# A quarter of a weight matrix decoded earlier, and lasting staging rooms, in a fused attention and two-MoE kernel

## The chip, the cores and the metric

One core of a Trainium2 chip runs the whole program. Engines are called as in the profile: PE (TensorE), DVE (VectorE), ACT (ScalarE), POOL (GpSimd), SP (SyncE, whose queue here issues all the large transfers). The metric is device time in microseconds (us) of one execution; lower is better.

## The reference

Three blocks follow each other; shapes are batch 4, 8 heads, S = 576, 2304 tokens of width 512.

```python
scores = q @ k.T / 8 + bias(pos)              # bias: small MLP of log distances, per head
x = softmax(scores) @ v                       # -> 2304 x 512
g = x @ w_gate; y = (silu(g) * (x @ w_val)) @ w_out       # MoE 1, 512 -> 1536 -> 512
h = relu(y @ w_in); out = (h * h) @ w_out2                # MoE 2, 512 -> 2048 -> 512
```

All tensors come as float64 in DRAM; the kernel sees the weights as pairs of 32-bit words.

## The kernel before, in words

**Stages.** Attention walks query tiles t = 0, 1, 2, 3 of 128 rows each and then a merged tile "m", made of the last 64 rows of two batches at a time. MoE 1 runs in nine units of 256 tokens, moe1(0) to moe1(8), mostly beside attention: per unit 12 steps f of 24 matmuls 128x128 by 128x256 (L460, gate and value), after each f a tanh on ACT (L468), two products on DVE (L469, L471) and, one step later, a cast on ACT (L445) and its remainder on POOL (L220); then 72 matmuls with the output weights (L483, "z times o"). MoE 2 follows for chunks of two units: hidden() is 192 matmuls (L1381) with elementwise work on ACT, POOL and DVE, outputs() is a scheme of 7 products (L1413) on combined weight blocks.

**Weights.** A weight block is 128 rows by 512 columns, 512 KB in DRAM. SP loads it raw into a staging room (`Source.load`, L283), DVE turns the word pairs into float32 with three instructions (`decode`, L262, L265, L267), ACT or POOL squares it and PE sums the squares for a norm (`first`, L328), and then `split` makes two float16 parts of it (L191 on DVE, L201, L205, L209 on ACT, L197 on POOL). w_in of MoE 2 has four column quarters of four blocks each, w_out2 has sixteen blocks (`second`, L361 for the squares). Quarters 0 and 1 of w_in are decoded in attention's merged tile, through rooms in `scrap`, into `room0` (w2a). When attention is over its pool is given back (`a_stack.close()` in `weights2`); a new pool holds `w2r` (25 blocks), `w2s` (three raw rooms) and `w2c`. Quarters 2 and 3 and then w_out2 pass through the three rooms. With all norms known, `combine(f)`, eight times, scales two blocks of w_out2 (L1212 on POOL, L1214 on ACT), takes differences (L1193) and casts (L1198 DVE, L1200 ACT) into C7. The hidden values of a chunk go to HS, MoE 1's outputs come back transposed as `yt` (`yt_load`, L1231), which in program order waits until gate and value of unit 8 are through, `("gv", 8)`.

**Tiles.** `room1` holds the score biases of an attention tile and `scrap` small tables and raw rooms; both belong to attention's pool before. In the merged tile only the first 4 S columns of `room1` hold biases, which the last softmax step (L823) of the tile reads.

**Order.** Generators for attention, weights and MoE 1 hand out costs at each `yield`; a merge with a table LEAD decides whose turn is next, and a scheduler then orders the instructions of each engine. Each engine runs its own queue in order. PSUM banks of MoE 1's steps: two buffers `mm`, and from the point where `w2r` exists every third step takes the single buffer `ma`.

## Time and profile before

| what | us |
|---|---|
| median of 3 runs | 1247.36 |
| lowest, highest | 1241.97, 1256.09 |
| profiled execution, its own time | 1245.34 |
| span of its trace | 1241.8 |
| PE busy | 1094.9 (88%) |
| DVE busy | 784.5 (63%) |
| ACT busy | 679.2 (55%) |
| POOL busy | 655.5 (53%) |
| mean granted TensorE clock | 0.954 |

The span runs from the first to the last instruction; the time has 3.5 us around it. PE is busiest over the whole, but a share of the whole mixes stages, so the rows below go stage by stage. Times in rows are us from the span's start. The merged tile runs from about 655 to 760, unit 7 from 751 to 806, unit 8 from 806 to 875, the first chunk of MoE 2 to 963.

### The profile page before, as it was taken

Reading aid. Unit: us, or ns where it says so; the run is one execution under the profiler, and the core shown is the slowest. Engines: PE = TensorE matmul, PEld = TensorE weight load, DVE = VectorE, ACT = ScalarE, POOL = GpSimd, SP = SyncE. Lnnn points to the kernel's source line nnn. Section 1 sums busy time; section 2 is a strip of 40 time slices with the busy share of each in tenths; the row PEclk is TensorE's granted clock in tenths of the full one; section 3 lists DMA queues with packets and bytes.
Section 4 is the critical chain, followed back from the end, with each engine's and each line's share of the span. In section 5 each row is a group of like instructions: output and inputs, shape, how many; then the busy total and the mean of one; then the engine's idle time right before and its main releaser. Section 6 shows DMA issues by size and latency. Waiting matters only on the chain.

```text
span 1241.8 us, 27334 instructions
## 1 busy us (share of the span) xinstructions
PE 1094.9 (88%) x10550; PEld 816.1 (66%) x10550; DVE 784.5 (63%) x1864; ACT 679.2 (55%) x1370; POOL 655.5 (53%) x835
## 2 busy tenths in 40 slices
PE   2587799998778889999997999979969999999998
PEld 2566688686467568686774767556438476584787
DVE  5989857887677667666665745885772442624423
ACT  3567767557566566566663543367551643616433
POOL 2433213279768587778794452227890542705423
PEclk9779899999879999999999999989979999999999
DMA  9957543219999998997989995660010010010100
GB/s 226 258 135 206 178 132 87 50 57 200 218 211 202 225 214 171 222 195 156 196 172 245 241 225 134 213 188 1 17 34 18 18 43 26 18 35 17 27 27 17
DMA packets 278078, 163.20 MB, mean 131 GB/s; under 512 B 233276, under 2 KB 246588, under 8 KB 277948
## 3 DMA queue, kind: packets, MB, share of 16 engines
q1 hardware_dynamic: 277948, 161.46, 55.4%
q8 instruction: 82, 1.34, 0.5%
q14 instruction: 48, 0.39, 0.1%
HBM read 92.13 MB, written 19.48 MB: 90 GB/s over the span
## 4 chain that ended last, share of the span: by engine, by line
PE 46%; DMA 15%; DVE 10%; POOL 8%; ACT 5%; issue 3%; SPq 1%; POOLq 0%; ACTq 0%; DVEq 0%
PE mm L1381 12%; PE mm L460 12%; PE mm L1413 11%; DMA pT<-pt 3%; PE mm L483 3%; POOL pt L220 2%; PE av L876 2%; PE ma L1413 2%; DMA qT<-qs 2%; PE qk L814 2%; DMA w2s<-in_moe_w_out_dram 2%; DMA scrap<-in_moe_w_in_dram 1%; POOL zx L1193 1%; DMA wr<-in_v_dram 1%; DMA w2s<-in_moe_w_in_dram 1%
## 5 line engine op out<-in xcount | busy, mean ns | idle before, releaser
L460 PEld LDWEIGHTS <-wr 128*128 128x128 f16 x2592 | 252.6, 100 | 52.8 <-issue 16.5
L1193 POOL TENSOR_TENSOR zx<-zx 128x256 f32<-128x256 f32 (+1 forms) x160 | 141.6, 895 | 181.6 <-ACT zx L1390 176.1
L460 PE MATMUL mm<-xT,wr 128*128 128x256 f16 x1536 | 184.1, 275 | 10.8 <-DVE th L471 5.2
L220 POOL TENSOR_TENSOR pt<-s,pt 128x512 f16<-128x512 f32 x224 | 173.6, 798 | 32.0 <-ACT pt L838 27.9
L220 POOL TENSOR_TENSOR zx<-th,zx 128x256 f16<-128x256 f32 x108 | 81.2, 754 | 129.9 <-ACT zx L445 126.0
L483 PE MATMUL mm<-wr,zx 128*128 128x512 f16 x612 | 142.3, 379 | 1.3 <-DVE th L471 1.3
L823 DVE CUSTOM_DVE_ANT_0 s<-qk,room 128x576 f32<-128x576 f32 x144 | 107.6, 748 | 40.2 <-PE qk L814 20.2
L1413 PEld LDWEIGHTS <-wr 128*128 128x128 f16 x1134 | 112.3, 99 | 27.0 <-DVE wr L1193 4.9
L1193 DVE TENSOR_TENSOR wr<-zx,wr 128x768 f16<-128x768 f32 (+3 forms) x60 | 78.3, 1312 | 61.9 <-ACT wr L1200 60.8
L831 ACT ACTIVATE s<-s,sc 128x576 f32<-128x576 f32 x112 | 85.5, 771 | 55.3 <-DVE sc L830 44.3
L460 PE MATMUL mm<-zx,wr 128*128 128x256 f16 x864 | 104.7, 278 | 2.4 <-DVE th L471 2.4
L606 DVE TENSOR_TENSOR scrap<-scrap,room 128x1024 f16<-128x1024 f16 (+1 forms) x108 | 87.8, 826 | 25.5 <-PE ma L645 21.3
L483 PEld LDWEIGHTS <-zx 128*128 128x128 f16 x648 | 60.1, 98 | 66.0 <-issue 2.4
L1381 PE MATMUL mm<-wr,room 128*128 128x512 f16 (+1 forms) x480 | 100.0, 358 | 0.0
L1381 PE MATMUL mm<-wr,w2r 128*128 128x512 f16 (+1 forms) x480 | 99.9, 358 | 0.0
L622 POOL TENSOR_TENSOR scrap<-scrap 128x256 f32<-128x256 f32 (+1 forms) x90 | 64.1, 713 | 65.9 <-ACT scrap L621 62.4
L876 PE MATMUL av<-vp,pT 128*128 128x65 f16 (+3 forms) x1792 | 70.5, 196 | 28.4 <-DMA pT<-pt 25.0
L876 PEld LDWEIGHTS <-pT 128*128 128x128 f16 (+1 forms) x1792 | 61.8, 102 | 43.5 <-DMA pT<-pt 33.2
L1432 ACT ACTIVATE ob<-ob,fac 128x256 f32<-128x256 f32 x36 | 17.8, 506 | 109.3 <-DVE ob L1431 109.3
L645 PEld LDWEIGHTS <-scrap 128*128 128x128 f16 x1440 | 60.3, 105 | 26.3 <-issue 11.9
L1381 PEld LDWEIGHTS <-w2r 128*128 128x128 f16 x480 | 47.0, 98 | 46.4
L1381 PEld LDWEIGHTS <-room 128*128 128x128 f16 x480 | 47.0, 98 | 45.5
(290 smaller groups left out, 2213.8 us busy)
## 6 DMA issues: line engine op xcount, KB each, us to landing
kp<-kT_d SPq DMA_DIRECT2D x64, 288.0 KB, 3.5
vp<-v_d SPq DMA_DIRECT2D x48, 325.0 KB, 3.5
w2s<-in_moe_w_out_dram SPq DMA_DIRECT2D x16, 512.0 KB, 3.9
wr<-in_moe_w_gate_dram SPq DMA_DIRECT2D x24, 256.0 KB, 5.0
wst<-in_moe_w_out_dram SPq DMA_DIRECT2D x12, 512.0 KB, 3.7
wr<-in_moe_w_val_dram SPq DMA_DIRECT2D x24, 256.0 KB, 4.2
...
```

The lines of the kernel that those rows point to most:

```text
L220: nc.gpsimd.tensor_tensor(out=out_, in0=x, in1=hi, op=ALU.subtract)
L460: nc.tensor.matmul(pg[:, 256 * gi:256 * gi + 256], wr.parts(key, f // 4, cc, wl, P * (f % 4), P), mov(xl, cc), start=k == 0, stop=k == 11)
L483: nc.tensor.matmul(po, zall[:, f, zl, P * t:P * t + P], wr.parts("o", 0, f, wl), start=k == 0, stop=k == 3 * NF1 - 1)
L606: nc.vector.tensor_tensor(out=m[:, :, ni * e:ni * e + ni], in0=block(kb, i0, ni), in1=th, op=ALU.is_gt)
L622: nc.gpsimd.tensor_tensor(out=tmp[r], in0=tmp[r], in1=xb, op=ALU.mult)
L645: nc.tensor.matmul(pv[:, :, :, c:c + 4], m[:, a, :], bd[:, l], start=l == 0, stop=l == 1)
L823: nc.vector.tensor_tensor_reduce(out=s.rearrange("p (a j) -> p a j", a=2), in0=pq[:, :, 0:288], in1=bias[:, n].rearrange("p (a j) -> p a j ...
L831: nc.scalar.activation(s, s, AF.Exp, bias=nm, scale=-1.0)
L876: nc.tensor.matmul(av[r, slot, 0:cn], pT[:, 5 * l + c, r], vs[e][c][:, c0:c0 + cn], start=m == 0, stop=m == 13)
L1193: (nc.gpsimd if how else nc.vector).tensor_tensor(out=out_, in0=a, in1=b, op=op)
L1381: nc.tensor.matmul(ph[:, :n], w2r.parts("w", g // 4, cc, wl, P * (g % 4), P), yt[:, 4 * yl + cc, :], start=m == 0, stop=m == 11)
L1413: nc.tensor.matmul(po, HS[f][:, o:o + P], st["C7"][f][wl][:, b:b + 256], start=f == 0 and k == 0, stop=f == 7 and k == 2)
```

## The change

`room1` and `scrap` move to the pool that lasts (`room1` shrinks to 4 S + 5 x 512 columns). Quarter 2 of w_in is now decoded before attention's pool is closed, into `w2b` behind the merged tile's biases; its raw blocks go through four rooms, two in `room1` in the place of these biases and two in `scrap`. Quarter 3 and w_out2 go through the same four rooms after the close, with four loads ahead instead of three, and the loads of w_out2 follow those of quarter 3 without a new start (`more`). `w2r` has 21 blocks, `w2s` and the tile `t` are gone, C7 and HS get other homes, and the wait `("gv", 8)` with `yt_load` stands at f = 6 instead of f = 5. Every instruction of before is still there, with the same shapes.

```diff
-    def first(ring, mats, cols, block, sg, ahead, mm, rooms=False):
+    def first(ring, mats, cols, block, sg, ahead, mm, rooms=False, more=()):
...
-            for j, key in order for kc in range(4) for i in range(512 // w)])
+            for j, key in order for kc in range(4) for i in range(512 // w)] + list(more))
+        st["so"] = so
...
+    def second_blocks(kc_n, src, w):
+        return [((kc, i), block_rows(src, w * i, kc, w)) for kc in range(kc_n) for i in range(512 // w)]
...
-        so = Source([
-            ((kc, i), block_rows(src, w * i, kc, w))
-            for kc in range(kc_n) for i in range(512 // w)])
+        so = st["so"] if later else Source(second_blocks(kc_n, src, w))
...
-    rooms = [gv.tile([P, BW], F32, name="room0"), att.tile([P, BW], F32, name="room1", bufs=1)]
+    rooms = [gv.tile([P, BW], F32, name="room0"), gv.tile([P, 4 * S + 5 * 512], F32, name="room1")]
...
+    w2b = rooms[1][:, 4 * S:4 * S + 5 * 512].rearrange("p (a b) -> p a b", b=512)
-    scrap = att.tile([P, 2112 + (TAB + TAB2) // 2], F32, name="scrap", bufs=1)
+    scrap = gv.tile([P, 2112 + (TAB + TAB2) // 2], F32, name="scrap")
+
+    def w2_place(j, kc):
+        if j < 2:
+            return w2a, 4 * j + kc, 1
+        return (w2b, 4 - kc, -1) if j == 2 else kc
...
-        t = st["w2p"].tile([P, 1024], F32, tag="t", name="t", bufs=1)
+        t = rooms[1][:, 1792:2816]
...
     def weights2():
+        sg2 = Stage(
+            512, [r[:, 1024 * i:1024 * i + 1024].bitcast(I64) for r in (rooms[1], scrap) for i in range(2)],
+            [scrap[:, 2048 + 256 * i:2304 + 256 * i].bitcast(BF16) for i in range(2)])
+        yield from first(
+            Ring(None, {"w": w2_place}), {"w": w2i}, range(2, 3), block_rows, sg2, 2, ma)
         a_stack.close()
...
-        w2s = w2p.tile([P, 3584], F32, name="w2s", bufs=1)
-        sg2 = Stage(
-            512, [w2s[:, 1024 * i:1024 * i + 1024].bitcast(I64) for i in range(3)],
-            [w2s[:, 3072 + 256 * i:3328 + 256 * i].bitcast(BF16) for i in range(2)])
-        yield from first(w2r, {"w": w2i}, range(2, 4), block_rows, sg2, 3, mm2)
+        yield from first(
+            w2r, {"w": w2i}, range(3, 4), block_rows, sg2, 4, mm2, more=second_blocks(NF2, w2o, 512))
...
-        yield from second(w2r, "2", NF2, w2o, kappa, sg2, 3, mm2, True)
+        yield from second(w2r, "2", NF2, w2o, kappa, sg2, 0, mm2, True)
...
-            if f == 5:
+            if f == 6:
                 yield ("gv", 8)
                 yt_load((0, 1))
```

SP's queue at the end of attention, before: the last three transposes `pT` (probabilities, for attention's last matmuls), MoE 1's output `y_d`, the transposes `xT` of unit 8's input, then all raw loads.

```order
L860 DMA_TRANSPOSE pT<-pt_124 128x9x128
L769 DMA vp<-v_d_70 128x1300
L860 DMA_TRANSPOSE pT<-pt_125 128x9x128
L769 DMA vp<-v_d_70 128x1300
L504 DMA y_d_77<-yh 128x1024
L769 DMA vp<-v_d_70 128x1300
L860 DMA_TRANSPOSE pT<-pt_123 128x9x128
L504 DMA y_d_77<-yh 128x1024
L929 DMA_TRANSPOSE xT<-xh 128x4x128 x4
L283 DMA w2s<-in_moe_w_in_dram 128x512 x8
L283 DMA w2s<-in_moe_w_out_dram 128x512 x11
```

The same place now (`room_119` is `room1`; four loads into `scrap` already stand further up, among the `kp` and `vp` loads of the merged tile):

```order
L283 DMA room_119<-in_moe_w_in_dram 128x512
L778 DMA vp<-v_d_70 128x1300
L869 DMA_TRANSPOSE pT<-pt_124 128x9x128
L283 DMA room_119<-in_moe_w_in_dram 128x512
L869 DMA_TRANSPOSE pT<-pt_125 128x9x128
L778 DMA vp<-v_d_70 128x1300
L283 DMA room_119<-in_moe_w_in_dram 128x512
L506 DMA y_d_77<-yh 128x1024
L869 DMA_TRANSPOSE pT<-pt_123 128x9x128
L778 DMA vp<-v_d_70 128x1300
L283 DMA room_119<-in_moe_w_in_dram 128x512
```

The loads into `room1` stand between the last `pT` transposes, and behind them come `xT` and then 16 loads of w_out2 alone.

DVE's queue in unit 7, before: one product of MoE 1 (`th`) follows each two or three decode instructions.

```order
L262 TENSOR_SCALAR w2r<-w2s 128x512
L469 SCALAR_TENSOR_TENSOR th<-th,ma 128x256
L265 SCALAR_TENSOR_TENSOR w2r<-w2s,w2r 128x512
L471 SCALAR_TENSOR_TENSOR th<-th,ma 128x256
L262 TENSOR_SCALAR w2r<-w2s 128x512
L267 SCALAR_TENSOR_TENSOR w2r<-w2s,w2r 128x512
L265 SCALAR_TENSOR_TENSOR w2r<-w2s,w2r 128x512
L469 SCALAR_TENSOR_TENSOR th<-th,mm 128x256
```

The same place now, the first `th` products of f = 6, 7 and 8:

```order
L265 SCALAR_TENSOR_TENSOR w2r<-room_119,w2r 128x512
L471 SCALAR_TENSOR_TENSOR th<-th,ma 128x256
L262 TENSOR_SCALAR w2r<-scrap 128x512
L471 SCALAR_TENSOR_TENSOR th<-th,mm 128x256
L150 TENSOR_SCALAR sc<-sc 1x1
L471 SCALAR_TENSOR_TENSOR th<-th,mm 128x256
L267 SCALAR_TENSOR_TENSOR w2r<-room_119,w2r 128x512
L191 SCALAR_TENSOR_TENSOR room_119<-room_119,keep_12234 128x512
L473 SCALAR_TENSOR_TENSOR th<-th,ma 128x256
```

Ahead of these rows stand the decodes of the four blocks of quarter 3 at once, with f = 5's products in their midst, and then those of five blocks of w_out2 without a `th` between them.

ACT's queue in unit 8, before, where the scaling of w_out2 blocks (L1214) begins behind the tanh of f = 8:

```order
L468 ACTIVATE th<-ma,ux 128x256
L445 CAST zx<-th 128x256
L468 ACTIVATE th<-mm,ux 128x256
L445 CAST zx<-th 128x256
L468 ACTIVATE th<-mm,ux 128x256
L1214 ACTIVATE w2r<-w2r,keep_12878 128x512 x11
L1200 CAST w2s<-w2r 128x256 x2
L445 CAST zx<-th 128x256
```

And now, where it begins behind the cast of f = 1:

```order
L470 ACTIVATE th<-ma,ux 128x256
L447 CAST zx<-th 128x256
L1223 ACTIVATE w2r<-w2r,keep_12877 128x512 x11
L470 ACTIVATE th<-mm,ux 128x256
L1209 CAST scrap<-w2r 128x256 x2
L1209 CAST room_119<-w2r 128x256
L1209 CAST scrap<-w2r 128x512 x2
L470 ACTIVATE th<-mm,ux 128x256
L1209 CAST room_119<-w2r 128x512
```

Ten of unit 8's twelve tanhs now stand among the casts of the combines; POOL's queue moves in the same way, with six of the eight combines, before two, ahead of the first differences of hidden().

## Rows read from the trace of the kernel before

**Rows 1.** Windows: length, then busy us (instructions) of each engine, clock, DMA share, GB/s.

```profile
700.00:767.00 67.00, 62.94 (x819) 44.49 (x817) 37.14 (x128) 32.58 (x69) 32.83 (x45) 1.00 0.81 192
751.00:790.00 39.00, 34.62 (x349) 29.17 (x342) 27.32 (x72) 15.08 (x36) 7.72 (x10) 1.00 0.51 144
806.00:853.00 47.00, 38.04 (x300) 31.06 (x299) 35.09 (x94) 31.73 (x72) 16.27 (x19) 0.89 0.43 129
821.30:826.70 5.40, 5.39 (x25) 3.73 (x25) 3.58 (x12) 2.68 (x6) 1.40 (x2) 0.50 1.04 344
845.00:934.00 89.00, 78.59 (x411) 41.47 (x409) 62.80 (x79) 54.55 (x92) 76.86 (x67) 0.90 0.08 18
910.00:934.30 24.30, 13.61 (x75) 8.48 (x72) 15.84 (x14) 13.30 (x19) 20.66 (x17) 0.65 0.21 43
915.50:932.50 17.00, 10.16 (x45) 6.11 (x45) 12.33 (x10) 7.89 (x12) 15.06 (x14) 0.50 0.04 8
963.00:1041.00 78.00, 78.00 (x529) 51.58 (x528) 31.69 (x35) 33.96 (x53) 30.54 (x32) 1.00 0.11 28
```

**Rows 2.** Chain of waits: start, us, what the end hung on.

```profile
933.20 1.05 ACT w2r L1200
934.30 1.70 PE mm L1413 x14
...
963.18 41.44 PE mm L1381 x192
```

**Rows 3.** PE's timeline in the first outputs(): idle before, and releaser, in brackets.

```profile
914.27 0.39 PE L1413 MATMUL ma<-wr 128*128 128x256 f16 x2 [2.59 <-ACT wr L1200]
917.71 0.39 PE L1413 MATMUL ma<-wr 128*128 128x256 f16 x1 [3.05 <-DVE wr L1193]
...
924.86 0.60 PE L1413 MATMUL mm<-wr 128*128 128x256 f16 x2 [3.56 <-DVE wr L1198]
```

**Rows 4.** PE's timeline in gate and value of unit 8.

```profile
810.03 0.37 PE L131 MATMUL mm<-ident,sc 128*1 128x128 f32 x1 [2.42 <-DVE sc L497]
...
821.31 4.00 PE L460 MATMUL ma<-xT,wr 128*128 128x256 f16 x18 [4.91 <-DVE sc L166]
...
833.91 2.78 PE L460 MATMUL mm<-xT,wr 128*128 128x256 f16 x24 [1.63 <-DVE th L471]
```

**Rows 5.** DVE's groups in 772 to 839.2: count, busy us, mean ns, idle before.

```profile
L265 DVE SCALAR_TENSOR_TENSOR w2r<-w2s,w2r 128x512 int32<-128x512 int32 x24 | 18.3, 761 | 0.1
L267 DVE SCALAR_TENSOR_TENSOR w2r<-w2s,w2r 128x512 int32<-128x512 int32 x24 | 16.9, 705 | 0.1
L262 DVE TENSOR_SCALAR w2r<-w2s 128x512 int32<-128x512 int32 x24 | 11.9, 495 | 8.6 <-DMA w2s<-in_moe_w_out_dram 4.2 <-DMA w2s<-in_moe_w_in_dram 4.1
```

**Rows 6.** DVE's timeline: last softmax step, first decode, scales known, two steps of unit 8.

```profile
744.35 0.76 DVE L823 CUSTOM_DVE_ANT_0 s<-qk,room 128x576 f32<-128x576 f32 x1
...
772.22 0.43 DVE L262 TENSOR_SCALAR w2r<-w2s 128x512 int32<-128x512 int32 x1 [3.00 <-DMA w2s<-in_moe_w_in_dram]
...
844.99 0.37 DVE L187 SCALAR_TENSOR_TENSOR keep<-keep,keep 128x1 f32<-128x1 f32 x4
...
856.34 0.42 DVE L469 SCALAR_TENSOR_TENSOR th<-th,mm 128x256 f32<-128x256 f32 x1 [0.78 <-ACT th L468]
...
863.44 0.41 DVE L469 SCALAR_TENSOR_TENSOR th<-th,mm 128x256 f32<-128x256 f32 x1
```

**Rows 7.** DMA issues in 680 to 940: count, KB each, median us to landing.

```profile
w2s<-in_moe_w_in_dram SPq DMA_DIRECT2D x8, 512.0 KB, 4.2
...
scrap<-in_moe_w_in_dram SPq DMA_DIRECT2D x3, 512.0 KB, 5.9
...
pT<-pt SPq DMA_TRANSPOSE x15, 4.3
```

**Rows 8.** POOL's differences of hidden(), in 845 to 934 and in 934 to 1197.

```profile
L1193 POOL TENSOR_TENSOR zx<-zx 128x256 f32<-128x256 f32 x32 | 32.4, 1028 | 1.4 <-ACT zx L1390 1.0
L1193 POOL TENSOR_TENSOR zx<-zx 128x256 f32<-128x256 f32 x96 | 91.0, 957 | 142.3 <-ACT zx L1390 138.5
```

More of the change, by code (lines that the diff above doesn't have):

```diff
@@ L229, in at @@
             w = self.place[key](j, kc)
-            return w if isinstance(w, tuple) else (self.t, w)
+            return w if isinstance(w, tuple) else (self.t, w, 1)
         def whole(self, key, j, kc):
-            t, i = self.at(key, j, kc)
-            return t[:, i + 1, :]
+            t, i, d = self.at(key, j, kc)
+            return t[:, i + d, :]
         def parts(self, key, j, kc, lo, c0=0, n=512):
             o = 512 * lo + c0
-            t, i = self.at(key, j, kc)
+            t, i, d = self.at(key, j, kc)
             return t.bitcast(F16)[:, i, o:o + n]
@@ L1173, in rest @@
                 gens.append((first(
-                    Ring(None, {"w": lambda j, kc: (w2a, 4 * j + kc)}), {"w": w2i}, range(2), block_rows, sg_e, 2, ma), 45.0))
+                    Ring(None, {"w": w2_place}), {"w": w2i}, range(2), block_rows, sg_e, 2, ma), 45.0))
             yield from merge(*gens)
@@ L1236, in weights2 @@
         ps2 = ctx.enter_context(tc.tile_pool(name="ps2", bufs=5, space=PSUM))
-        w2r = Ring(w2p.tile([P, 25, 512], F32, name="w2r", bufs=1), {
-            "w": lambda j, kc: (w2a, 4 * j + kc) if j < 2 else 4 * j - 8 + kc, "2": lambda j, kc: 8 + kc})
+        w2r = Ring(w2p.tile([P, 21, 512], F32, name="w2r", bufs=1), {
+            "w": w2_place, "2": lambda j, kc: 4 + kc})
         st["w2p"], st["ps2"], st["w2r"] = w2p, ps2, w2r
@@ L1253, in weights2 @@
             kappa.append(kap)
-        yield from second(w2r, "2", NF2, w2o, kappa, sg2, 3, mm2, True)
-        new = w2p.tile([P, 3584], F16, name="w2c", bufs=1)
-        w2h, wrh, w2sh = [t.rearrange("p a b -> p (a b)").bitcast(F16) for t in (
-            w2r.t, wr.t, w2s.rearrange("p (a b) -> p a b", a=7))]
+        yield from second(w2r, "2", NF2, w2o, kappa, sg2, 0, mm2, True)
+        new = w2p.tile([P, 1792], F16, name="w2c", bufs=1)
+        w2h, wrh = [t.rearrange("p a b -> p (a b)").bitcast(F16) for t in (w2r.t, wr.t)]
+        sch, r1h = scrap.bitcast(F16), rooms[1].bitcast(F16)
         def rooms2(t, a, b=None):
@@ L1263, in rooms2 @@
             return t[:, a:a + 1792], t[:, b:b + 1792]
-        st["C7"] = [rooms2(w2sh, 0), rooms2(w2sh, 3.5), rooms2(w2h, 9, 17), rooms2(new, 0), rooms2(w2h, 11, 19),
-                    rooms2(wrh, 4), rooms2(wrh, 7.5), rooms2(wrh, 11)]
-        st["HS"] = [wrh[:, int(1024 * o):int(1024 * o) + 3584] for o in (15, 18.5, 22, 25.5, 29, 32.5)] + [
-            w2h[:, 1024 * o:1024 * o + 3584] for o in (13, 21)]
+        st["C7"] = [rooms2(sch, 0), (sch[:, 3584:5376], new), rooms2(w2h, 5, 13), rooms2(r1h, 0), rooms2(w2h, 7, 15),
+                    rooms2(w2h, 9, 17), rooms2(wrh, 4), rooms2(w2h, 11, 19)]
+        st["HS"] = [wrh[:, int(1024 * o):int(1024 * o) + 3584] for o in (7.5, 11, 15, 18.5, 22, 25.5, 29, 32.5)]
         st["yt"] = wrh[:, 0:4096]
         for f in range(8):
-            if f == 5:
+            if f == 6:
                 yield ("gv", 8)
```

## The prediction, made before the result was known

> **What bounds the kernel now.** I first read the chain of waits from its end backwards. It ends in pure PE work: behind a last ACT cast at 933.20 nothing but matmuls stands in it, to the end of the span [rows 2]. So the last 308 us are PE's own; what can be won lies ahead of 934.3, and it is won only where PE waits or runs slowly. Next I read windows by stage [rows 1]. From 963 to 1041, a steady chunk of MoE 2, PE is busy 78.00 of 78.00 at clock 1.00, and all others under half. From 910 to 934.3, the first outputs(), PE is busy 13.61 of 24.30 at clock 0.65: it waits for combined blocks, as the brackets in PE's timeline name them (wr from ACT and DVE, 2.59, 3.05 and 3.56 us) [rows 3]. In 845 to 934 POOL is busy 76.86 of 89.00: combines and hidden differences together. In gate and value of unit 8, 806 to 853, PE is busy 38.04 of 47.00 at 0.89, and the brackets name DVE (2.42, 4.91, 1.63 us) [rows 4], which decodes there. Ahead of that, 700 to 767 has PE at 62.94 of 67.00 and a DMA share of 0.81: the merged tile is near what the transfers allow. So the chain that matters is decode, scales, combines, outputs. The first decode of quarter 2 begins at 772.22, 28 us after the last softmax step (744.35); the scales are known at 844.99 and outputs() flows at 934.3, 89 us later [rows 2, 6].
>
> **What the change moves.** Four of the 24 blocks that DVE decodes between 772 and 839 go ahead of it, into the merged tile. A block costs 18.3 + 16.9 + 11.9 us over 24, so 1.96 us of DVE [rows 5]: 7.8 us less there. The fourth room and the unbroken row of loads take at most the 8.6 us that DVE spent waiting for loads [rows 5]. Together at most 16.4; I take 15, so scales at about 830 by DVE alone. All else that POOL, ACT and DVE do behind the scales is as much as before: 830 + 89 = 919 for outputs() to flow, if the order behind is as good.
>
> The terms, each against PE's path of before:
>
> (a) First outputs(). 73 matmuls run in the 24.4 us from 909.87 to 934.30; at 0.109 us each (41.44 / 192 is 0.216 for 512 columns [rows 2], half of it for 256) they want 8.0. If combines come in time, −16.4. POOL's order puts six combines ahead of the hidden differences, so they should.
>
> (b) Unit 8. 288 matmuls at 0.109 are 31.4 us, and it took 46.2 from 806.68 to 852.89; 30 small ones stay, say 0.8. Half the decodes that blocked DVE there now lie earlier, and the slow stretches at clock 0.50, one of them 821.3 to 826.7 [rows 1], each came right behind a PE idle time. −14.0.
>
> (c) Unit 7 gets what unit 8 loses. In the order of DVE the first products of f = 6, 7 and 8 stand behind nine decodes in a block. PE has three banks, so it can be at most three steps ahead of DVE. Four blocks of quarter 3 at once are 7.8 us of DVE, beside 24 matmuls that take 2.78 [rows 4]; walking the queue step by step I get stalls of 3.4 before f = 6, 2.9 before f = 9 and 6.1 before f = 10, and about 4 us at half clock behind them, for such idle times brought it in [rows 1, 4]: 16.4, against 3.4 us of unit 7's idle that go (751 to 790 has PE at 34.62 of 39.00 [rows 1], the rest of which lies in attention's end). +13.
>
> (d) The merged tile. Four more raw loads of 512 KB and a wait: the loads into room1 in SP's queue wait for the last softmax steps, which read the biases there, and behind them stand the last transposes pT, for which PE waits. A load lands in 5.9 us there [rows 7], a pT in 4.3. From below 0: the last pT could have issued at 749.16 only when its own input was there. From above 8: two loads' 5.9 us less the 4 us that PE has in hand with gate and value of unit 7. Nothing in the order gives a gain. The two loads that can start early are few, so I take the lower third, +3.
>
> (e) yt now waits at f = 6, and the order puts unit 8's first 31 hidden matmuls behind it inside unit 8: +1.3, between 0 and 5, a transpose's landing [rows 7], the matmuls of unit 8 cover most.
>
> (f) PE's path would then be at its outputs() before POOL's 919: +2.
>
> Sum −16.4 − 14.0 + 13 + 3 + 1.3 + 2 = −11.1. The profiled execution took 1245.34, so 1234.2; the median of the runs is 2.0 higher, so **1236**. All runs lie within 1241.97 to 1256.09.
>
> One row is weighed against a rule. POOL's differences of hidden took 1028 ns in 845 to 934, where DVE computes differences too, and 957 ns later [rows 8], 7% more in company. The Trainium skill, page "SBUF — State Buffer", section Who interferes with whom, says that a DVE instruction with two SBUF inputs contends with a POOL instruction that reads SBUF. By it, the combines that now meet DVE's products in unit 8 would go slower, and scales to flow would be a few us more than 89. The rows bear out its direction and give a bound: 7% of POOL's 76.86 us is 5.4; term (f) would rise by that, the sum to −6.
>
> **The rivals.**
>
> *Full gain (1223).* The DVE order in unit 7 costs nothing, because the loads of quarter 3 come one by one at 4.2 us [rows 7] and the products slip between them. Then (c) is 0: 1236 − 13 = 1223. For it: decodes before waited for loads, 8.6 us. Against it: the engine keeps its order, and a `th` behind a decode waits for that decode's load too. Chance 0.27.
>
> *My forecast (1236).* Chance 0.40, of which 0.18 ends more than 1% faster and 0.22 within it.
>
> *No change (1247).* Unit 7's stalls and the merged tile take it all: (c) 20, with each stall at the 4.91 us of the largest seen [rows 4], and (d) at 8. −16.4 − 14 + 20 + 8 + 1.3 + 2 = +1: 1246 for the profiled execution, 1248 against the median, 1247 between them. Such a result also comes where outputs() would never wait again but PE's own work decides. Beside it stands the Trainium skill, page "Perfetto Trace Analysis", section Identifying the Most-Contended Engine: the engine with the highest occupancy is to be worked on first. In 845 to 934 that is PE, 78.59 against POOL's 76.86, whose work is unchanged; by that rule nothing is won there. The brackets speak against it: PE's busy time there holds slow matmuls, at clock 0.50 in 915.5 to 932.5 [rows 1], and waits stand between them. Chance 0.15.
>
> *Slower (1266).* The combines now lie inside unit 8, on the engines that its f steps need: ACT has 11 scalings and casts before most tanhs, POOL the combines before the remainders, and DVE its products between differences. Where combines and steps met before, f = 10 and f = 11 were 7.1 us apart (856.34 to 863.44 [rows 6]), against 2.78. Unit 8 begins at 806.7 + 13 + 3 = 822.7; four steps last until 834, 31 hidden matmuls until 842, then 7.1 us a step as long as the combines last. If these take the 89 us less the 32.4 of hidden's differences [rows 6, 8], they end at 830 + 57 = 887; that is 6.3 steps, and the other 1.7 at 2.78 end at 892. Then 72 matmuls (15.5), 161 of hidden (34.8) and 73 of outputs (8.0) end at 950, 16 us behind 934.3; with 3 for half clock +19: 1264, or 1266 against the median. It decides from a spacing of about 3.9 us on: with 8 × 3.9 = 31 unit 8 ends at 873 and all of it at 931, plus the 3. Against it: in ACT's order the last tanh of unit 8 stands behind the cast of the fourth combine, and four combines are half of POOL's 76.86 − 32.4 = 44.5 us [rows 1, 8], 22 us for ten steps, under the 27.8 that PE itself takes for them; the remainders of the steps come on top, and waits of one engine for another. Chance 0.18.
>
> That the change doesn't do what it says is part of the forecast: blocks 2 and 3 of quarter 2 can load early, into scrap, but the other two only behind the last softmax step. If quarter 2 were decoded only where before quarter 2 was, the first term of the 15 us falls to 4 and the sum rises by about 4.
>
> **How the numbers follow.** A measurement of this kernel cannot tell under about 1% from no change: 1234.9 to 1259.8. Faster: 0.27 + 0.18 = 0.45; same: 0.22 + 0.15 + 0.02 = 0.39; slower: 0.16, the slower case without a tenth of it that stays inside the bound. Range: from full gain with (d) at 0, 1220, less one, to the lower end of the slower case, 1262, with a spacing of 6.4 us: 1219 to 1262, which leaves out some 0.1 above and some 0.05 below. The forecast's own range is 1228 to 1244: (c) between 5 and 20.
>
> **What would show it.** In the trace after: the first outputs() without idle above 1 us and at clock 1.00 (a); unit 8's gate and value in about 32 us plus the hidden matmuls (b); idle time on PE in unit 7 with DVE's product as releaser, some 12 us, and a stretch at 0.50 (c); first pT behind a room1 load later than its input (d); scales at 830 instead of 845. I am wrong if scales come at 840 or later (decode is bound by loads), if unit 8's steps are 5 us apart (slower case), or if unit 7 runs without stalls (full gain).

## The result: half a per cent slower, and the profile after

| what | before | after |
|---|---|---|
| median, 22 runs each, us | 1245.72 | 1252.05 |
| lowest to highest of the change's runs | | 1246.79 to 1257.67 |
| ratio to before, with 95% interval | | 1.0052 [1.0036, 1.0067] |
| profiled execution, us | 1245.34 | 1252.81 |
| span of its trace, us | 1241.8 | 1249.3 |

The kernel became 6.3 us slower. The forecast was 1236, 0.8% faster than these runs of before. The result lies inside the range, and within the 1% that was called no change, but on the other side than forecast.

**One moment for all traces.** A profile is one execution, and the part of the program that the change leaves alone shifts between profiles: the same softmax step, ahead of any moved instruction, starts at 604.38 in before and 605.61 in after, and between 600.6 and 611.0 over all traces here. Below, every moment is counted from that step. Before, in DVE's timeline (start, us, engine, line, operation, out<-in, count), with two rows of the first outputs() that are needed further on:

```profile
604.38 0.74 DVE L823 CUSTOM_DVE_ANT_0 s<-qk,room 128x576 f32<-128x576 f32 x1
...
916.18 1.47 DVE L1193 TENSOR_TENSOR wr<-zx,wr 128x768 f16<-128x768 f32 x1
...
923.60 1.21 DVE L1198 CAST wr<-zx 128x1024 f16<-128x1024 f32 x1
```

After, DVE's timeline: that step; the first decode of quarter 2; the last softmax step of the merged tile; the last decode of quarter 2; `xh`, the input of the transposes `xT`; the first decode into `w2r`; the scales; two rows of outputs(). They answer to [rows 6] and to the fence above.

```profile
605.61 0.74 DVE L832 CUSTOM_DVE_ANT_0 s<-qk,room 128x576 f32<-128x576 f32 x1
...
707.46 0.41 DVE L262 TENSOR_SCALAR room<-scrap 128x512 int32<-128x512 int32 x1
...
751.04 0.76 DVE L832 CUSTOM_DVE_ANT_0 s<-qk,room 128x576 f32<-128x576 f32 x1
...
759.09 0.43 DVE L262 TENSOR_SCALAR room<-room 128x512 int32<-128x512 int32 x1 [4.26 <-DMA room<-in_moe_w_in_dram]
...
774.69 1.67 DVE L935 SCALAR_TENSOR_TENSOR xh<-x,ux,xh 128x256 f16<-128x256 f32 x4
...
783.62 0.76 DVE L262 TENSOR_SCALAR w2r<-room 128x512 int32<-128x512 int32 x2 [3.35 <-DMA xT<-xh]
...
841.46 0.37 DVE L187 SCALAR_TENSOR_TENSOR keep<-keep,keep 128x1 f32<-128x1 f32 x4
...
925.63 1.53 DVE L1202 TENSOR_TENSOR wr<-zx,wr 128x768 f16<-128x768 f32 x1 [0.80 <-ACT wr L1209]
...
934.90 0.56 DVE L1207 CAST wr<-zx 128x768 f16<-128x768 f32 x1
```

Quarter 2's four blocks are decoded from 707.46, 713.75, 748.48 and 759.09 on: two inside the merged tile and two at its end. Counted from the common step the first is 66 us earlier than in [rows 6] (101.9 against 167.8). But the last softmax step is 5.4 us late (751.04 − 605.61 = 145.4, against 744.35 − 604.38 = 140.0), and the first decode into the new pool waits for a transpose `xT` and starts 10.2 us later than before's first (178.0 against 167.8). After, in SP's timeline:

```profile
750.85 0.34 SPq L283 DMA_DIRECT2D room<-in_moe_w_in_dram  x1
751.29 2.30 SPq L869 DMA_TRANSPOSE pT<-pt  x1
...
754.30 0.38 SPq L283 DMA_DIRECT2D room<-in_moe_w_in_dram  x1
...
761.90 0.33 SPq L283 DMA_DIRECT2D room<-in_moe_w_in_dram  x1
770.13 0.34 SPq L506 DMA_DIRECT2D y_d<-yh  x1
775.20 5.13 SPq L938 DMA_TRANSPOSE xT<-xh  x4
```

and before:

```profile
761.19 5.12 SPq L929 DMA_TRANSPOSE xT<-xh  x4
```

The raw loads stand ahead of the transposes, and the last transposes begin 12.8 us later from the common step (169.6 against 156.8). At the end it is not SP's queue that holds them: SP stood idle from 770.47 to 775.20, until DVE had written the first `xh`. Attention's last matmuls began 6.8 us late (156.2 against 149.4); the rest arose between them and `xh`. Windows after (length, busy us and instructions of PE, PEld, DVE, ACT and POOL, clock, DMA share, GB/s): the last 20 and the last 10 us ahead of attention's last matmuls, unit 7, gate and value of unit 8, from the scales to outputs(), the first outputs(), and a stretch of unit 7:

```profile
741.80:761.80 20.00, 17.50 (x232) 10.36 (x229) 11.16 (x37) 7.04 (x13) 8.99 (x11) 0.99 0.88 229
751.80:761.80 10.00, 7.50 (x97) 4.80 (x95) 5.06 (x15) 3.30 (x5) 5.30 (x6) 0.98 1.00 257
755.80:816.30 60.50, 42.89 (x386) 34.23 (x385) 43.25 (x116) 26.87 (x61) 16.24 (x14) 0.83 0.52 154
831.90:873.30 41.40, 39.75 (x327) 31.67 (x326) 24.15 (x62) 25.69 (x55) 27.69 (x29) 1.00 0.20 39
841.80:939.40 97.60, 89.81 (x548) 52.80 (x546) 61.70 (x88) 59.88 (x105) 79.22 (x74) 0.98 0.13 25
923.90:943.00 19.10, 12.39 (x85) 8.51 (x84) 11.33 (x11) 9.33 (x15) 11.32 (x11) 0.82 0.29 55
...
806.10:810.20 4.10, 4.10 (x24) 3.02 (x24) 4.10 (x9) 1.18 (x3) 3.87 (x4) 0.61 0.39 131
```

Before, the last 20 and the last 10 us ahead of attention's last matmuls:

```profile
733.80:753.80 20.00, 20.00 (x245) 10.89 (x243) 8.15 (x31) 6.41 (x12) 9.74 (x13) 1.00 0.90 199
743.80:753.80 10.00, 10.00 (x136) 5.82 (x130) 5.10 (x15) 3.30 (x5) 5.80 (x8) 1.00 0.72 153
```

Over the 20 us the DMA share is the same, 0.90 and 0.88; over the last 10 it went from 0.72 to 1.00. Unit 8 now runs nearly full, 39.75 of 41.40 at clock 1.00, where before it was 38.04 of 47.00 at 0.89 [rows 1]. Unit 7 is what unit 8 was: 42.89 of 60.50 at 0.83. PE's timeline after shows where:

```profile
761.83 0.98 PE L885 MATMUL av<-vp,pT 128*64 128x65 f16 x28 [2.34 <-DMA vp<-v_d]
763.86 4.95 PE L462 MATMUL mm<-xT,wr 128*128 128x256 f16 x24 [1.05 <-DVE th L473]
...
770.16 3.11 PE L462 MATMUL mm<-xT,wr 128*128 128x256 f16 x27 [1.25 <-DVE sc L150]
...
789.35 0.27 PE L329 MATMUL mm<-ones_b,scrap 128*128 128x1 bf16 x4 [5.00 <-ACT scrap L325]
...
806.08 4.33 PE L462 MATMUL ma<-xT,wr 128*128 128x256 f16 x24 [5.84 <-DVE th L473]
...
927.22 0.28 PE L1423 MATMUL ma<-w2r,wr 128*128 128x256 f16 x1 [1.17 <-DVE wr L1202]
...
935.52 0.59 PE L1423 MATMUL ma<-w2r,wr 128*128 128x256 f16 x2 [2.24 <-DVE wr L1207]
```

Waits of 5.00 and 5.84 us stand in unit 7. The 24 matmuls behind the wait of 5.84 take 4.33 us, and those behind 2.34 and 1.05 take 4.95, instead of 2.78 [rows 4]; the granted clock from 806.1 to 810.2 is 0.61, so most of it lies at the lower level of 1.2 GHz. In outputs() the releasers are DVE's `wr<-zx` instructions, as before. The chain of waits after ends as in [rows 2], 7.5 us later in the trace and 6.3 us later from the common step (365.1 against 358.8):

```profile
939.37 3.82 PE mm L1423 x20
```

```profile
970.70 41.44 PE mm L1391 x192
```

Stage by stage, us from the common step. The idle columns are sums of the brackets on PE: "unit 7" from the wait ahead of attention's last matmuls to the wait ahead of unit 7's z times o, that one included; "unit 8" from there to outputs(), so with hidden(); "outputs()" from there to the second chunk. Rows below the second give differences to before; one profile each.

| kernel | last `xT` | z times o, unit 7 | scales | outputs() | second chunk | idle: unit 7, unit 8, outputs() |
|---|---|---|---|---|---|---|
| before | 156.8 | 185.9 | 240.6 | 305.5 | 358.6 | 4.4, 9.0, 10.7 |
| after | +12.8 | +24.9 | −4.8 | +12.8 | +6.3 | 17.5, 2.4, 6.7 |
| e1 | −0.1 | +23.9 | −7.6 | +9.9 | +4.4 | 20.8, 0.7, 7.3 |
| e2 | +13.9 | +19.4 | −1.7 | +14.0 | +8.4 | 14.4, 5.7, 7.1 |
| e3 | +5.8 | +17.7 | −12.0 | +5.8 | +0.7 | 14.9, 2.4, 7.4 |
| e5 | +8.2 | +13.5 | −2.4 | +9.4 | +2.9 | 10.3, 7.4, 6.5 |
| e6 | +0.4 | +10.0 | −4.4 | +9.0 | +3.7 | 10.5, 7.7, 7.4 |
| f1 | +7.3 | +15.1 | −14.9 | +3.2 | −3.4 | 12.4, 1.3, 7.4 |
| g1 | +6.0 | +8.6 | −8.4 | +3.5 | −1.2 | 5.4, 6.3, 8.5 |
| g2 | −0.7 | −1.9 | +12.4 | +7.3 | +8.4 | 3.1, 16.8, 11.1 |
| g3 | +0.8 | +7.0 | −21.6 | −5.5 | −12.7 | 8.5, 2.2, 5.9 |
| h1 | 0.0 | 0.0 | −3.2 | +2.1 | −0.6 | 4.3, 11.7, 9.4 |
| h2 | −0.3 | +18.8 | −3.8 | +11.6 | +5.4 | 16.2, 5.5, 7.1 |
| h3 | +2.5 | +3.8 | −11.6 | +0.2 | −8.6 | 4.5, 7.4, 5.4 |

**What one profile cannot tell.** Six kernels are equal up to attention's end (before, e8, g1, g2, h1, h3), and yet their last `xT` lies between −1.7 us (e8) and +6.0 us (g1) from that of before. The five that load all of quarter 2 early in after's places (after, e4, e5, f1, f2) have +7.3 to +12.8. So the early loads and decodes cost time there, but up to 6 us of any one row may be chance.

### The profile page after: what moved, and what is told of

Its sections match the earlier page's. It is cut to its first block, busy times and chain, and to the rows that moved or that the text cites. A ratio compares the mean times of both kernels' runs of the same rounds, so it can differ in the third digit from the quotient of the medians.

```text
span 1249.3 us, 27327 instructions
## 1 busy us (share of the span) xinstructions
PE 1099.8 (88%) x10550; PEld 818.1 (65%) x10550; DVE 777.9 (62%) x1864; ACT 680.0 (54%) x1370; POOL 658.5 (53%) x835
## 4 chain that ended last, share of the span: by engine, by line
PE 42%; DMA 13%; DVE 12%; POOL 10%; ACT 6%; issue 4%; SPq 2%; POOLq 0%; DVEq 0%; ACTq 0%
PE mm L1391 12%; PE mm L1423 11%; PE mm L462 10%; DMA pT<-pt 3%; POOL pt L220 3%; PE mm L485 2%; DMA qT<-qs 2%; POOL zx L1202 2%; PE ma L1423 2%; DMA scrap<-in_moe_w_in_dram 2%; PE qk L823 1%; DMA wr<-in_v_dram 1%; PE av L885 1%; DVE s L832 1%; DMA xT<-xh 1%
## 5 line engine op out<-in xcount | busy, mean ns | idle before, releaser
L462 PEld LDWEIGHTS <-wr 128*128 128x128 f16 x2592 | 255.7, 101 | 61.0 <-issue 21.0
L462 PE MATMUL mm<-xT,wr 128*128 128x256 f16 x1584 | 195.3, 280 | 10.5 <-DVE th L473 5.1
L220 POOL TENSOR_TENSOR pt<-s,pt 128x512 f16<-128x512 f32 x224 | 173.5, 797 | 25.6 <-ACT pt L847 22.0
L1423 PEld LDWEIGHTS <-wr 128*128 128x128 f16 x1512 | 148.3, 98 | 27.6 <-DVE wr L1202 4.3
L1202 DVE TENSOR_TENSOR wr<-zx,wr 128x768 f16<-128x768 f32 (+1 forms) x80 | 98.0, 1237 | 80.6 <-ACT wr L1209 79.3
L1391 PE MATMUL mm<-wr,room 128*128 128x512 f16 (+1 forms) x720 | 143.6, 358 | 1.1 <-ACT zx L1396 0.7
L485 PE MATMUL mm<-wr,zx 128*128 128x512 f16 x576 | 134.8, 380 | 1.3 <-DVE sc L839 1.3
L832 DVE CUSTOM_DVE_ANT_0 s<-qk,room 128x576 f32<-128x576 f32 x144 | 107.7, 749 | 43.9 <-PE qk L823 24.9
L1391 PEld LDWEIGHTS <-room 128*128 128x128 f16 x720 | 70.3, 98 | 70.1 <-issue 1.6
L462 PE MATMUL mm<-zx,wr 128*128 128x256 f16 x864 | 108.2, 283 | 3.0 <-DVE th L473 3.0
L615 DVE TENSOR_TENSOR scrap<-scrap,room 128x1024 f16<-128x1024 f16 (+1 forms) x108 | 88.1, 829 | 21.9 <-PE ma L654 18.8
L1423 PE MATMUL mm<-w2r,wr 128*128 128x256 f16 x636 | 95.7, 274 | 2.5 <-DVE wr L1202 1.3
L654 PEld LDWEIGHTS <-scrap 128*128 128x128 f16 x1440 | 60.3, 105 | 28.9 <-issue 13.9
L823 PEld LDWEIGHTS <-qT 128*128 128x128 f16 x512 | 49.1, 102 | 36.8 <-issue 12.7
```

What stands on the lines that cost most here:

```text
L220: nc.gpsimd.tensor_tensor(out=out_, in0=x, in1=hi, op=ALU.subtract)
L462: nc.tensor.matmul(pg[:, 256 * gi:256 * gi + 256], wr.parts(key, f // 4, cc, wl, P * (f % 4), P), mov(xl, cc), start=k == 0, stop=k == 11)
L485: nc.tensor.matmul(po, zall[:, f, zl, P * t:P * t + P], wr.parts("o", 0, f, wl), start=k == 0, stop=k == 3 * NF1 - 1)
L615: nc.vector.tensor_tensor(out=m[:, :, ni * e:ni * e + ni], in0=block(kb, i0, ni), in1=th, op=ALU.is_gt)
L823: nc.tensor.matmul(pq[:, j, 0:288], qT[:, 2 * (n % 4) + s, :], kts[0][:, js], start=s == 0, stop=s == 1)
L832: nc.vector.tensor_tensor_reduce(out=s.rearrange("p (a j) -> p a j", a=2), in0=pq[:, :, 0:288], in1=bias[:, n].rearrange("p (a j) -> p a j ...
```

## The experiments

Each is timed against before on the same chip; a ratio above 1 is slower. The base is the kernel after, unless the label says before. q2 is quarter 2. Of each edit the lines that carry it are shown.

### Where the raw loads stand: e1, e2, e3

Theory A: the loads spoil attention's end, and all else follows. Theory B: DVE's decode is only moved.

**e1**, all raw loads of q2, q3 and w_out2 behind the last `xT` (`last_t`):

```diff
+                with tc.issue_after(last_t[0].ins) if "sg2" in st else ExitStack():
+                    for i, a in enumerate(ap):
+                        nc.sync.dma_start(r[n * i:n * i + n], a)
```

> Every raw load of quarters 2 and 3 is put behind the last transposes xT in SP's queue; all else as in the changed kernel. Theory A (the eight loads in SP's queue ahead of the last pT and xT, and DVE's waits for them, move attention's end, on which w2r opens): xT issues at about 761 again instead of 775, the last scale comes near 840, and the time falls to 1238 to 1246, at or below the kernel before. Theory B (the four rooms, the other homes, or POOL's and ACT's work of unit 8 behind the scales cost the time, wherever attention ends): it stays at 1250 to 1254.

1.0045 [1.0021, 1.0070], 1253.43 us. In SP's timeline of e1 the transposes are back in their place (156.7 us behind the common step):

```profile
765.18 5.12 SPq L941 DMA_TRANSPOSE xT<-xh  x4
```

but PE's idle in unit 7 is as long in sum (20.8 us against 17.5 in after); its two largest groups (engine, line, waited for, us in total, times, longest):

```profile
PE mm L332 <- ACT scrap L328: 6.3, 4, 2.4
PE ma L465 <- DVE th L476: 4.2, 1, 4.2
```

Attention's end is as before and the loss stays: theory A as the only cause falls.

**e2**, q2 behind the last `pT`, the rest behind `xT`:

```diff
+                with tc.issue_after(last_t[key[0] != 2].ins) if "sg2" in st else ExitStack():
```

> Quarter 2's four loads stand behind the last pT in SP's queue, quarter 3's behind the last xT. Theory A: attention's end as before the change (xT near 761 to 763), quarter 2 decoded by 766, scales near 832, and 1232 to 1240, faster than both kernels. Theory B: 1250 to 1254.

1.0040 [1.0016, 1.0065], 1250.62 us. With q2 behind `pT` alone `xT` is still 13.9 us late; in e6, below, which differs from e2 in DVE's order alone (decodes held behind `th` and `xh`), it is not. So in e2 it is decodes on DVE ahead of `xh` that hold `xT`, not the loads' place in SP's queue.

**e3**, q2's loads bring a quarter of the bytes, which the decode reads four times; q2's weights are not the reference's:

```diff
+                    c = 128 if small else 512
+                    nc.sync.dma_start(r[n * i:n * i + n, 0:c], a[:, 0:c])
```

> Quarter 2's four early loads bring 128 of 512 columns each, and its decode reads these four times over, so 1.5 MB less go in the merged tile while every instruction stays; quarter 2's weights are not those of the reference. If the bytes are what moves attention's end (DMA share was already about 1.0 there): xT 5 us earlier or more, 1245 to 1248. If it is the places in the queues and the waits: xT within 2 us of 775, 1250 to 1253.

0.9998 [0.9975, 1.0020], 1246.80 us. The loss is gone, and in this profile `xT` is 5.8 us late and the scales come 12 us early. That lighter loads shorten attention's end is not shown: with all bytes `xT` is 7.3 to 8.5 us late in f1, f2 and e5, with a quarter of them 8.0 in f3 below, and with no early load at all 6.0 in g1. That bytes explain the whole loss is contradicted by e1.

### Where DVE's and POOL's steps stand: e4 to e8

**e4**, remainders of unit 8 on DVE:

```diff
+                (nc.vector if m == 8 else nc.gpsimd).tensor_tensor(
+                    out=zall[:, f, 1, :], in0=th, in1=zall[:, f, 0, :], op=ALU.subtract)
```

> The twelve remainders of unit 8 are computed on DVE instead of POOL; all else as in the changed kernel. If POOL bounds the stretch from the scales to the first outputs() (97.6 us against 89.3 before, with 7.8 us of such remainders against 2.6), about 5 us less: 1246 to 1249. If that stretch is bound by PE or by waits of one engine for another: 1250 to 1254.

1.0042 [1.0017, 1.0068], 1251.93 us: POOL's remainders behind the scales are not the price, for the interval lies on that of after.

**e5**, each decode behind the last product `th` written ahead of it in the program:

```diff
+            for n in (("th",) if "sg2" in st else ()):
+                es.enter_context(tc.issue_after(st[n].ins))
```

> DVE's queue is held to the order of the program: each decode of quarters 2, 3 and w_out2 stands behind the last products of MoE 1 written before it. All else as in the changed kernel. Theory C (unit 7's stalls come from products that stand behind decodes in DVE's queue; from the start of unit 7 to z times o 60.5 us against 38.5 before the change): 8 to 12 us less in unit 7, and 1240 to 1246. Theory D (the stalls come from PE's own norm matmuls and from loads, or what follows the scales is bound by ACT and POOL anyway): 1249 to 1253.

1.0005 [0.9984, 1.0025], 1248.96 us. Unit 7's idle falls from 17.5 to 10.3, and unit 8's rises from 2.4 to 7.4. In PE's timeline of e5:

```profile
799.95 8.11 PE L488 MATMUL ma<-wr,zx 128*128 128x512 f16 x29 [4.21 <-DVE th L476]
...
827.98 2.29 PE L465 MATMUL mm<-xT,wr 128*128 128x256 f16 x10 [5.29 <-DVE sc L502]
```

The first wait stands at unit 7's own z times o. The second stands in unit 8: the decodes that gave way in unit 7 now block it there.

**e6**, e2 and e5 together, and decodes also behind `xh`, the input of `xT`:

```diff
+            for n in (("th", "xh") if "sg2" in st else ()):
+                es.enter_context(tc.issue_after(st[n].ins))
```

> Quarter 2's loads behind the last pT, the later ones behind the last xT, and in DVE's queue each decode behind the last products of MoE 1 written before it and behind attention's last normalisation xh. Theories A and C together: xT at 761 to 764, quarter 2 decoded between 762 and 772 where DVE was idle before, unit 7 short, 1230 to 1240. Theory D: 1247 to 1253.

0.9990 [0.9964, 1.0016], 1247.12 us. Attention's end as before (`xT` +0.4), no loss, and no gain: idle 10.5, 7.7, 7.4.

**e7**, e1 with e6's order on DVE:

```diff
+                with tc.issue_after(last_t[0].ins) if "sg2" in st else ExitStack():
...
+            for n in (("th", "xh") if "sg2" in st else ()):
```

> As the run with all loads behind xT (1253.4), with DVE's decodes held behind the products of MoE 1 as well. Nothing of quarter 2 is early then, so it is the kernel before with four rooms and other homes. Theory C: unit 7's 20 us of idle halve, 1240 to 1247. Theory D: 1250 to 1254.

1.0034 [1.0010, 1.0058], 1250.03 us: with no early load, DVE's order gives back nothing that can be told from e1.

**e8**, e5's order in before:

```diff
+            for n in (("th",) if "sg2" in st else ()):
+                es.enter_context(tc.issue_after(st[n].ins))
```

> The kernel before the change with the same hold on DVE's decodes. Its products stood between decodes already in unit 7, so theory C expects little: 1242 to 1249. If it falls under 1240, the order of DVE is worth time without the rest of the change.

1.0001 [0.9978, 1.0023], 1245.46 us: nothing to win there.

### The length of decode and hidden's differences: f1 to f4

**f1**, L267 left out for q2, q3 and w_out2 (their three lowest bits are missing, here and in g1, g3, h3):

```diff
+        if "sg2" not in st:
+            nc.vector.scalar_tensor_tensor(
```

> The changed kernel with the third instruction of the decode (L267) left out for quarters 2, 3 and w_out2, 20 of them behind attention's end and 4 before: these weights lack their three lowest bits. It takes about 0.7 us x 24 = 17 us from DVE. If DVE's decode is what unit 7 and the scales wait for (theory E): scales near 830 instead of 841.5, unit 7's stalls smaller, 1238 to 1246. If the transfers or PE's own order set the pace: 1249 to 1253.

1.0005 [0.9984, 1.0027], 1246.88 us: 0.47% below after.

**f2**, in chunk 0 the second difference of each step of hidden() (S3) always goes to DVE (0), instead of the turn that `mixed` gives:

```diff
+        def how(i):
+            return mixed("s") if c or i != 1 else 0
```

> The changed kernel with one of the four differences of hidden() on DVE instead of POOL, in the first chunk alone: 8 of 32, about 8 us off POOL between the scales and the first outputs(). If POOL's work behind the scales is what makes outputs() wait (6.7 us of stalls and half clock): 1244 to 1249. If the waits are for the last steps' own latency or PE's path: 1250 to 1253.

1.0024 [1.0001, 1.0047], 1249.47 us; idle in outputs() 5.6 instead of 6.7. A small part, if any: the intervals of f2 and after overlap.

**f3**, e3 and e5 together (q2's weights as in e3):

```diff
+                    c = 128 if small else 512
...
+            for n in (("th",) if "sg2" in st else ()):
```

> Both single edits that helped, together: a quarter of the bytes of quarter 2's loads (its weights are not the reference's), and decodes behind the products of MoE 1 in DVE's queue. Alone they gave ratios of 0.9998 and 1.0005 to the kernel before, against 1.0052 of the changed kernel. If bytes and DVE's order are two separate causes they add: ratio 0.993 to 0.997, 1237 to 1243. If both only move the same idle time of PE to another place: 0.998 to 1.001, 1244 to 1248.

1.0052 [1.0021, 1.0083], 1253.05 us. Each alone gave the loss back, both together do not: idle 14.1 in unit 7 and 7.1 in unit 8, 27.5 with outputs(), against 24.2 in e5. Its interval and that of e5 overlap from 1.0021 to 1.0025 only. That was expected by no theory and stays open.

**f4**, e6 and f2 together:

```diff
+            for n in (("th", "xh") if "sg2" in st else ()):
...
+            return mixed("s") if c or i != 1 else 0
```

> A version that computes the reference and may beat both: loads of quarter 2 behind the last pT, the others behind the last xT, decodes behind the products of MoE 1, and one of the four differences of the first chunk on DVE. From 1247.1 for the same without the differences: 1241 to 1245 if POOL holds outputs() up, else 1245 to 1249.

0.9990 [0.9968, 1.0013], 1245.10 us, the ratio of e6: on top of it the differences give nothing that these runs can tell.

### A dose of decode: g1, g2, g3

**g1**, before with f1's decode; **g2**, before with L267 done twice:

```diff
+        if "sg2" not in st:
```

> The kernel before the change, the third instruction of the decode (L267) left out for quarters 2, 3 and w_out2 (three lowest bits of these weights). 17 us less on DVE between attention's end and the scales. If DVE's decode sets the pace before the change too: scales near 833 instead of 845, 1234 to 1241. If it is hidden there by transfers and PE: 1243 to 1248.

```diff
+        for _ in range(2 if "sg2" in st else 1):
```

> The kernel before the change with that third instruction done twice (the second leaves the value as it is) for the same 24 blocks: 17 us more on DVE. If DVE's decode sets the pace: scales near 860, 1252 to 1263. If there is room on DVE: 1244 to 1249.

g1 0.9952 [0.9932, 0.9972], 1240.45 us; g2 1.0066 [1.0041, 1.0092], 1253.79 us. The 16.9 us of L267 [rows 5] removed or added move the scales by −8.4 and +12.4 and the time by −0.48% and +0.66%. Counted from the last `xT`, which in g1 happened to come 6.0 us late and in g2 0.7 early, the scales moved by −14.4 and +13.1: most of the dose, both ways. DVE's rows of the scales, g1:

```profile
840.27 0.37 DVE L187 SCALAR_TENSOR_TENSOR keep<-keep,keep 128x1 f32<-128x1 f32 x4
```

and g2:

```profile
855.79 0.37 DVE L187 SCALAR_TENSOR_TENSOR keep<-keep,keep 128x1 f32<-128x1 f32 x4
```

In g2, PE's timeline names DVE as what it waited for in unit 8, and the 24 matmuls behind take 5.09 us instead of 2.78:

```profile
818.12 5.09 PE L461 MATMUL ma<-xT,wr 128*128 128x256 f16 x24 [7.19 <-DVE th L472]
```

So DVE's decode paces the stage in before already, and f1 and g1 win the same from it, with the change and without it.

**g3**, f4 with f1's decode:

```diff
+        if "sg2" not in st:
...
+            return mixed("s") if c or i != 1 else 0
```

> The version with loads at two places, decodes behind the products of MoE 1 and one of four differences of the first chunk on DVE (ratio 0.999 to the kernel before), with the two-step decode. Relief on DVE was worth 5 us in the changed kernel; here 1236 to 1242, below both kernels, if it adds; 1243 to 1247 if not.

0.9890 [0.9866, 0.9914], 1231.65 us, faster than both kernels. Its windows of unit 7, of gate and value of unit 8 and of the first outputs():

```profile
752.00:797.00 45.00, 36.47 (x360) 30.32 (x358) 31.50 (x95) 22.53 (x51) 11.95 (x14) 1.00 0.60 193
812.00:853.00 41.00, 38.80 (x323) 31.23 (x322) 25.22 (x66) 27.66 (x59) 26.27 (x27) 1.00 0.23 61
903.80:923.00 19.20, 13.34 (x92) 9.74 (x91) 11.77 (x13) 8.66 (x14) 9.37 (x9) 0.82 0.26 55
```

The clock is 1.00 in both units, and 0.82 in the first outputs(), as in after. The idle of all three parts is 16.6 us, against 24.0 in before and 26.5 in after.

### Which part of the change: h1, h2, h3

**h1**, before with a fourth raw room and unbroken loads, no quarter moved:

```diff
+        w2s = w2p.tile([P, 4096], F32, name="w2s", bufs=1)
...
+        yield from first(w2r, {"w": w2i}, range(2, 4), block_rows, sg2, 4, mm2, more=second_blocks(NF2, w2o, 512))
```

> The kernel before the change with a fourth raw room and w_out2's loads straight behind those of w_in (ahead 4); homes and everything else as before. If the four rooms let decodes crowd ahead of MoE 1's products and so cost the time: 1249 to 1253. If they only shorten the decode: 1238 to 1245.

0.9988 [0.9969, 1.0007], 1242.03 us: the scales come 3.2 us earlier and nothing comes of it.

**h2**, e1 with three rooms and the loads of w_out2 started apart:

```diff
-            ... for r in (rooms[1], scrap) for i in range(2)],
+            ... for r in (rooms[1], scrap) for i in range(2)][:3],
...
-        so = st["so"] if later else Source(second_blocks(kc_n, src, w))
+        so = Source(second_blocks(kc_n, src, w))
```

> The version with all raw loads behind xT (1253.4, ratio 1.0045) with three rooms and three loads ahead again, w_out2's loads started apart: of the change only the other homes and lasting tiles are left. If the rooms were the cost: 1244 to 1248. If the homes or the wait at f = 6: 1250 to 1254.

1.0059 [1.0036, 1.0083], 1253.27 us. Neither the early loads nor the fourth room are in it; the lasting tiles, the homes, the place of q2 in the program and the wait at f = 6 are, and the loss is whole. PE's waits in its unit 7:

```profile
PE mm L332 <- ACT scrap L328: 4.2, 2, 3.1
PE ma L465 <- DVE th L476: 3.2, 1, 3.2
```

PE's queue stands for the squares of norms, and a step's bank waits for DVE. A trait that fits, argued and not tested: q2 now stands in the program ahead of the point from which every third step takes bank `ma`, so unit 7 uses `ma` for fewer matmuls and shares it with q2's norms. Before, 751 to 806:

```profile
L460 PE MATMUL ma<-xT,wr 128*128 128x256 f16 x96 | 11.4, 272 | 0.0
```

and after, 755 to 832:

```profile
L462 PE MATMUL ma<-xT,wr 128*128 128x256 f16 x48 | 7.2, 317 | 6.8 <-DVE th L473 5.8 <-DVE keep L297 0.9
```

96 of 288 against 48. Which of the remaining differences makes h2's cost stays open.

**h3**, before with f1's decode and f2's differences:

```diff
+        if "sg2" not in st:
...
+            return mixed("s") if c or i != 1 else 0
```

> The kernel before the change with the two-step decode (alone 0.9952) and one of four differences of the first chunk on DVE: what the best version (0.989) has beside the change and its orders. If the early quarter, rooms and orders are worth something once DVE is relieved: 1237 to 1241. If not: 1230 to 1234.

0.9902 [0.9870, 0.9935], 1234.92 us. Its interval overlaps g3's: of g3's gain, the moved quarter has no part that these runs can tell. The gain comes from the shorter decode and perhaps the differences (h3's interval touches that of g1, which has the decode alone).

## Why the prediction was wrong, point by point

Moments from the common step; time differences against before.

**The step that failed** is "all else behind the scales is as much as before: 830 + 89 = 919", and with it (a). From the scales to flowing outputs() it was 97.9 us and not 89.3, and from the scales to the second chunk 129.1 us and not 118.0. The scales came at 841.46 and not at 830, which the prediction itself gave as its refutation, but not for the reason given there, a decode bound by loads. From the first decode behind attention to the scales it took 57.8 us against 72.8 in before, so the 15 us were saved there; but that decode started 10.2 us later, counted from the common step, and the scales are 4.8 us early instead of 15. Of the 17.4 us between the forecast sum and the measured one, (a) is 10.0.

- **(a) First outputs(), −16.4 forecast, −6.4 measured** (from its start to the second chunk, 53.1 to 46.7 us). The rows were misread. The names `wr` in the brackets of [rows 3] were taken for combined blocks; but hidden values lie in `wr` as well. Of before, the product at 916.18 ends at 917.65 and PE goes at 917.71; the cast at 923.60 ends at 924.81 and PE goes at 924.86. Both read `zx`: they are hidden values, as is ACT's cast ahead of 914.27. Earlier combines could shorten these waits only where a combine stood ahead of a hidden value on DVE, ACT or POOL; they could not remove them. After, the same two lines still release PE (1.17 and 2.24 us), and all eighteen kernels of the experiments kept 5.4 us of idle or more in that part.
- **(b), (e) Unit 8, −12.7 forecast, −11.3 measured** (52.7 to 41.4 us from its gate and value to z times o; `yt` waits 0.36). The mechanism held, clock 1.00 included.
- **(c) Unit 7, +13 forecast, +18.1 measured** (attention's last matmuls to z times o, 36.4 to 54.5 us). The sum of the stalls is as the walk along DVE's queue gave it, 5.00 + 0.35 + 0.42 + 0.94 + 5.84 = 12.6 against 3.4 + 2.9 + 6.1 = 12.4, but partly by luck: 5.8 of it stands at the matmuls of a norm, which waited for squares on ACT and which the walk did not have, and DVE's products released one long stall, 5.84, instead of three. The term mis-sized is the half clock: about 4 us were allowed, and a clock of 0.83 over 60.50 us costs 10.3. Waits of 1.05 and 1.25 where attention ends were lacking too.
- **(d) The merged tile, +3 forecast, +6.8 measured** (its last matmul). The bounds, 0 to 8, held, and whether the lower third was wrong one profile cannot tell: e4, e5, f1 and f2, with the same loads, have +5.0, +5.4, +4.6 and +3.0, and g1, which changes nothing up to there, +6.0. The term left out what comes next: the last `xT` was 12.8 us late, and the new pool, so all of quarter 3's decode, waits for it (3.35 us at 783.62).
- **(f), +2 forecast.** PE's path and POOL's were to meet; the excess behind the scales is unit 8's work that now lies there. POOL's remainders are not its price (e4).

The measured sum: +6.8 + 18.1 − 0.9 (z times o of unit 7) − 11.3 + 0.0 (from unit 8's z times o to outputs(), 50.5 in both) − 6.4 = +6.3. That this is also 1252.05 − 1245.72 is chance, for each term is of one profile. The rival "no change" came nearest, with (c) 20 and (d) 8; its error is the same (a).

**Under the terms.** The work was not shortened. The idle of PE in the three parts is 24.0 us in before, 26.5 in after, and 24 to 29 in e1 to e8, f2 to f4, h1 and h2. Within that band it goes with the time: the kernels that lose 0.3% or more (after, e1, e2, e4, e7, f3, h2) have 26.1 to 28.8 us, those with a ratio up to 1.0024 (e3, e5, e6, e8, f2, f4, h1) 24.2 to 25.6. Kernels with a shorter decode have less (g1 20.2, f1 21.1, h3 17.2, g3 16.6), the one with a longer decode more (g2 31.0). With four blocks of decode moved ahead of attention's end, the idle moved from unit 8 into unit 7; e5 carries part of it back. The dose (g1, g2) shows that this decode sets the pace; e1, h1 and h2 show that neither the early loads nor the fourth room alone make the loss. The loss of 0.5% beyond that isn't settled whole: with attention's end restored and decodes held back it is gone (e6, 0.9990), with attention's end restored by late loads alone it stays (e1, 1.0045), and held decodes added to that give little (e7, 1.0034).

**Two rules.** By the Trainium skill, page "Perfetto Trace Analysis", section Identifying the Most-Contended Engine, the engine with the highest occupancy comes first, which by matmul time would be PE in 806 to 853 (38.04 against DVE's 35.09 of 47.00 [rows 1]). But that page makes an exception of TensorE: its matmul busy time is no good measure, and among what is to be taken instead is the busy share of the weight loads (PEld). That is 31.06 us in 806 to 853, under DVE's 35.09, and 41.47 in 845 to 934, under POOL's 76.86 [rows 1]; so the prediction's rival applied the rule to a figure that the page excludes. Read so, the rule names DVE in 806 to 853, and the runs agree: taking work from DVE won 0.48% (g1). The other, the Trainium skill's page "SBUF — State Buffer", section Who interferes with whom, had put up to 5.4 us on (f) for combines that meet DVE's products. But these products read one input from the PSUM banks `mm` and `ma`, and the rule is of two SBUF inputs. POOL's differences of hidden, and two groups of its combines, after from 841.8 to 939.4 (count, busy us, mean ns, idle before):

```profile
L1202 POOL TENSOR_TENSOR zx<-zx 128x256 f32<-128x256 f32 x32 | 32.9, 1042 | 5.2 <-ACT zx L1400 4.2
...
L1202 POOL TENSOR_TENSOR room<-w2r 128x256 f32<-128x256 f32 x5 | 4.2, 846 | 0.1
L1202 POOL TENSOR_TENSOR room<-w2r,room 128x256 f32<-128x256 f32 x5 | 4.0, 797 | 0.9 <-DVE sc L150 0.5 <-DVE room L1202 0.4
```

and the same combines before, from 845 to 934:

```profile
L1193 POOL TENSOR_TENSOR t<-w2r 128x256 f32<-128x256 f32 x5 | 5.9, 1181 | 0.1
L1193 POOL TENSOR_TENSOR t<-w2r,t 128x256 f32<-128x256 f32 x5 | 5.5, 1101 | 1.6 <-DVE t L1193 1.6
```

The differences of hidden took 1042 ns in the mean against 1028 [rows 8], so 32 of them lost 0.4 us, and these combines became faster: the cost of up to 5.4 us did not come.
